# The second half of head 0's keys in one transfer instead of two

## The chip, the cores and the metric

The kernel runs on 1 core of one Trainium2 chip. The metric is the time of one execution on the device in microseconds (us). Before the change it is 656.38 us, the median of 3 runs (656.35 to 656.39).

## What is computed

One token passes through a decoder layer: layer norm, attention over a long cache, and a gated feed-forward block. The part that matters here is the attention. 32 query heads share 8 key-value heads, each with 65536 cached rows of 128 bf16 numbers, 16 MB of keys and 16 MB of values a head:

```python
B, Sq, D = 1, 1, 512
Hq, Hkv, Sk, Dh = 32, 8, 65536, 128
q = (x @ wq).reshape(B, Sq, Hq, Dh).transpose(0, 2, 1, 3)
scores = jnp.einsum("bhqd,bhkd->bhqk", q, k) * (Dh ** -0.5)
p = _softmax(scores, axis=-1)
o = jnp.einsum("bhqk,bhkd->bhqd", p, v)
# then o @ wo, the residual, layer norm, sigmoid(g) * u and the down projection
```

Every byte of the cache is read once.

## The kernel before, in words

**Tiles.** The 16 MB of one head's keys (or values) are 32 chunks. A chunk is 2048 bf16 numbers (4 KB) on each of 128 partitions. Keys and values arrive in `ring`, a buffer of 36 chunks. A load normally brings half a head: 16 chunks, 64 KB on each partition, 8 MB in all. The two halves are called `Kh.0`, `Kh.1`, `Vh.0`, `Vh.1` for head h.

**Engines.** VectorE turns each chunk of keys with one 32x32 block transpose (L531, `ktw<-ring`) into `ktw`, which holds 8 chunks. TensorE then multiplies the query into it, four matmuls a chunk (L443, `PS<-ktw`). It does this in groups of four chunks, and a place in `ktw` is free for the transpose eight chunks later when the scores of its chunk are done. After the 32 chunks of a head comes the softmax: VectorE takes the maxima (L538 and L562 to L568), ScalarE the exponentials (L577) and the next head's query weights (L500). The values are multiplied (L443, `PS<-ring,PT_sb`) during the next head, half a head at a time, after the second and the fourth quarter of that head's keys.

**The order of the loads.** All of them are issued by SyncE (SP) from one list written out by hand, and SP works strictly in its order (L339 to L375). A load that writes over a part of `ring` waits for a mark that the part has been read. The marks of the keys are tiny memsets behind the transposes (L534). In head 0, mark `F0.0` stands after the first 16 chunks and `F0.1` after all 32. In the later heads the marks `Fh.0` and `Fh.1` stand after 12 and 28 chunks. `PVh.r` is the end of the value matmuls in quarter r. The list begins so:

| load | place in `ring` | SP waits for |
|---|---|---|
| `wq` (4 MB, into `ktw`), `K0.0a`, `K0.0b`, `K0.1a`, `K0.1b` (4 MB each) | chunks 0 to 35 | nothing |
| `K1.0` | 0 to 15 | `F0.0` |
| `V0.0` | 20 to 35 | `F0.1` |
| `K1.1` | 4 to 19 | `F1.0` |
| `V0.1` | 20 to 35 | `PV0.1` |
| `K2.0`, then on in the same way | 0 to 15 | `F1.1` |

**Head 0.** Its keys come in four loads of eight chunks, each with a semaphore of its own. `ORDER` (L247) says in which order the chunks are turned: 4 to 15, then 0 to 3, then 16 to 31. So the transposes number s = 0, 4, 16 and 24 of head 0 are the ones that wait for `K0.0a`, `K0.0b`, `K0.1a` and `K0.1b` (L524). Transpose s = 0 waits for the query as well. The later heads have two waits, at s = 0 and s = 16.

Of the kernel before, what the change touches and what calls it, by code (L numbers as in the profile page):

```python
# [35 lines left out]
class Prog:  # L36
# [14 lines left out]
    def op(self, eng, fn, deps=(), name=None, to=None, times=1):  # L51
        assert name is None or name not in self.where, name
        self.ops[eng].append(dict(fn=fn, deps=[d for d in deps if d], name=name, dma=None, to=to, times=times, part=self.part.get(eng)))
        if name:
            self.where[name] = (eng, len(self.ops[eng]) - 1)

    def dma(self, eng, fn, sem, deps=(), name=None):
        self.op(eng, fn, deps, name)
        rec = self.dma_sems.setdefault(sem, dict(sem=None, count=0))
        rec["count"] += 16  # L60
        self.ops[eng][-1]["dma"] = (sem, rec["count"])
# [162 lines left out]
def bass_sequential_preLN__gqa_block_cached__glu_gated_glu__decode_kernel(  # L224
# [22 lines left out]
    with ExitStack() as es:  # L247
# [67 lines left out]
        def ps(bank, c0, c1, p0=0, p1=128):  # L315
            return PS[p0:p1, bank * 512 + c0: bank * 512 + c1]
# [13 lines left out]
        def first_chunk(k, h, q):  # L330
            return AT[{("K", 0): "K0", ("V", HKV - 1): "V7"}.get((k, h), k)][q]

        def load(k, h, q, deps, sem, name, cols=None):
            j0, j1 = PIECES[q]
            a, z = cols or (j0, j1)
            cache = A_k_cache if k == "K" else A_v_cache
            rows = cache[0, h, j0 * TC * 128:j1 * TC * 128, :].rearrange("(p t) d -> p (t d)", p=128)
            at = (first_chunk(k, h, q) - j0) * CH
            dma("sp", lambda e: e.dma_start(ring[:, at + a * CH:at + z * CH], rows[:, (a - j0) * CH:(z - j0) * CH]), sem, deps, name)  # L339

        dma("sp", lambda e: e.dma_start(ktw[:, 0:NKT * CH].rearrange("p (k n) -> p k n", k=4),
                                        A_wq.rearrange("(p k) n -> p k n", p=128)), "r0", (), "wq")
        for q in range(2):
            for i in range(2):
                j0 = 16 * q + 8 * i
                load("K", 0, q, (), f"r{2 * q + i + 1}", f"K0.{q}{'ab'[i]}", (j0, j0 + 8))
        for h in range(1, HKV):
            load("K", h, 0, ["F0.0" if h == 1 else f"F{h - 1}.1"], "ka", f"K{h}.0")
            load("V", h - 1, 0, ["F0.1" if h == 1 else f"PV{h - 2}.3"], "va", f"V{h - 1}.0")
# [164 lines left out]
        def dve_block(b):  # L514
            h, r = b // NR, b % NR
            for c in range(NC):
                n, s = b * NC + c, r * NC + c
                j = ORDER[s]
                q = sum(j >= z for _, z in PIECES)
                at = (first_chunk("K", h, q) + j - PIECES[q][0]) * CH  # L520
                src = ring[:, at:at + CH].bitcast(fp32)
                dst = ktw[:, (n % NKT) * CH:(n % NKT + 1) * CH].bitcast(fp32)
                if h == 0:
                    deps = [f"K0.{q}{'ab'[j % 16 // 8]}"] if s in (0, 4, 16, 24) else []  # L524
                    if s == 0:
                        deps.append("q")
                else:
                    deps = [f"K{h}.{q}"] if s in (0, 16) else []
                if r:
                    deps.append(f"S{b - 1}.{c}")  # L530
                op("dve", lambda e, d=dst, sr=src: e.transpose(d, sr), deps, f"T{b}.{c}", to="T")  # L531
                mark = ({15: 0, 31: 1} if h == 0 else {11: 0, 27: 1}).get(s)
                if mark is not None:
                    op("dve", lambda e, m=4 * h + mark: e.memset(scr[:, m:m + 1], 0.0), (), f"F{h}.{mark}")  # L534
            if b % NR == NR - 1:
                for k in range(NR):
                    u = b - NR + 1 + k
                    op("dve", lambda e, u=u: e.tensor_reduce(M_sb[:, u % 4:u % 4 + 1], ps(u % NS, 0, 512), AX.X, ALU.max),  # L538
                       [f"S{b}.{NC - NR + k}"], f"mx{u}", to="D")
                op("dve", lambda e: e.memset(scr[:, 32 + b // NR:33 + b // NR], 0.0), (), f"G{b // NR}")  # L540
# [255 lines left out]
        for i in range(HKV + 1):  # L796
            loop, last = 0 < i < HKV, i == HKV
            for r in range(NR):
                P.part = {"dve": (f"A{r}", i) if loop else None}
                if not last:  # L800
                    dve_block(NR * i + r)
                    pe_scores(NR * i + r)
                if i and r == 1:
                    P.part = {"dve": ("A4", i) if loop else None}
                    transposed(i - 1)
                    P.part = {"pe": ("V0", i), "dve": ("B0", i) if loop else None}
                    denominators(i - 1)
                    op("pe", lambda e: None, [f"V{i - 1}.0", f"z{i - 1}"])
                    pv(i - 1, r, 6)
                    pv(i - 1, r, 2)  # L810
                if i and r == 3:
                    if last:
                        P.part["pe"] = ("L", i)
                        project7()
                        columns()
                    P.part["pe"] = ("V3", i)
                    op("pe", lambda e: None, [f"V{i - 1}.1"])
                    pv(i - 1, r, 5 if last else 6)
                    if last:
                        P.part["pe"] = ("VL", i)  # L820
                        op("pe", lambda e: None, [f"V{i - 1}.1b"])
                    pv(i - 1, r, 3 if last else 2)
                    P.part["pe"] = ("O", i)
                    head_out(i - 1)
                if not last and r == 3:
                    P.part = {"pe": ("X", i), "dve": ("A3", i) if loop else None}
                    softmax(i)
# [89 lines left out]
```

## Time and profile before

| what | us |
|---|---|
| median of 3 runs | 656.38 (656.35 to 656.39) |
| span of the profiled execution, first to last instruction | 655.0 |
| of the median outside that span | 1.4 |
| TensorE busy in the span | 397.5 |
| VectorE busy | 350.3 |
| ScalarE busy | 43.1 |
| bytes read from HBM | 282.33 MB |

Of the profiled execution the page gives the span, and no other time of its own, so its time is set beside the median as span plus 1.4 us. Times inside the trace are counted from the span's start. PE is TensorE, PEld its weight loads, DVE VectorE, ACT ScalarE, SPq the issuing sequencer of SyncE. In the rows on DMAs the last column is the time from issue to landing, that is until the semaphore of the load is full. In the timelines the columns are start, length, engine, line, operation and tiles.

### The profile page before, as it was taken

The numbers are of one execution on the slowest core, as the hardware profiler recorded it, in microseconds if no ns is written. First come the engines' busy times: TensorE is split into PE (matmuls) and PEld (weight loads), VectorE is DVE, ScalarE is ACT, GpSimd is POOL, SyncE is SP. The second block draws the span as 40 slices with busy tenths as digits, with TensorE's granted clock in tenths as the row PEclk, the third lists the DMA queues.
The fourth block names the chain that finished last, engine by engine and source line by source line (L and its number), as shares of the span: only waits on it lengthen the run. The fifth ranks groups of instructions, "written<-read, shape, count | busy, mean of one in ns | idle before, by whom it ended". The sixth has DMA issues, their size and how long they took to land.

```text
span 655.0 us, 6176 instructions
## 1 busy us (share of the span) xinstructions
PE 397.5 (61%) x2317; PEld 66.7 (10%) x1549; DVE 350.3 (53%) x428; ACT 43.1 (7%) x114; POOL 3.7 (1%) x19
## 2 busy tenths in 40 slices
PE   2778672937548293674828467392845739285466
PEld 1100010110101000010100101010010101001122
DVE  3398853819266290935719184481917548092202
ACT  1100200020000200002000200002000020001101
POOL 1000000000000000000000000000000000000000
PEclk9799695977959687785968769596796958878656
DMA  9999999999999999999999999999999989999998
GB/s 400 432 434 462 424 408 448 448 448 412 420 448 448 432 400 448 448 448 404 428 448 448 436 396 448 448 448 416 416 448 448 448 384 448 448 448 424 417 412 363
DMA packets 6372, 282.33 MB, mean 431 GB/s; under 512 B 738, under 2 KB 868, under 8 KB 1252
## 3 DMA queue, kind: packets, MB, share of 16 engines
q1 hardware_dynamic: 6340, 282.33, 99.7%
q10 hardware_dynamic: 32, 0.00, 0.0%
HBM read 282.33 MB, written 0.00 MB: 431 GB/s over the span
## 4 chain that ended last, share of the span: by engine, by line
DMA 66%; DVE 30%; PE 2%; issue 1%; SPq 0%; PEldq 0%
DMA ring<-in_A_k_cache_dram 58%; DVE ktw L531 30%; DMA ring<-in_B_w_up_dram 4%; DMA ring<-in_A_v_cache_dram 4%; PE PS L443 2%; PE PS L866 0%; PE PS L847 0%; DVE hh L859 0%; DVE hhT L863 0%; SPq L368 0%; SPq L339 0%; DVE y_sb L884 0%; PEldq L171 0%
## 5 line engine op out<-in xcount | busy, mean ns | idle before, releaser
L531 DVE STREAM_TRANSPOSE ktw<-ring 128x1024 f32<-128x1024 f32 x256 | 291.5, 1208 | 165.0 <-DMA ring<-in_A_k_cache_dram 165.0
L443 PE MATMUL PS<-ktw 128*128 128x512 bf16 x1024 | 276.3, 419 | 163.4 <-DVE ktw L531 155.8
L443 PE MATMUL PS<-ring,PT_sb 128*32 x1024 | 85.0, 420 | 55.0 <-issue 46.6
L443 PEld LDWEIGHTS PS<-ktw 128*128 x256 | 26.2, 102 | 401.5 <-issue 234.3
L618 ACT ACTIVATE po_sb<-PS,rl 128x512 bf16<-128x512 f32 x8 | 5.5, 687 | 523.4 <-PE PS L443 523.4
L443 PEld LDWEIGHTS PS<-ring,PT_sb 128*32 x1024 | 20.7, 116 | 117.5 <-issue 116.2
L566 DVE TENSOR_REDUCE gmj<-PS 1x4 f32<-1x128 f32 x8 | 2.2, 278 | 53.5 <-PE PS L564 53.5
L538 DVE TENSOR_REDUCE M_sb<-PS 128x1 f32<-128x512 f32 x32 | 19.9, 683 | 19.3 <-PE PS L443 19.3
L577 ACT ACTIVATE P_sb<-PS,negmax 128x512 bf16<-128x512 f32 x32 | 21.6, 686 | 0.3
L587 DVE STREAM_TRANSPOSE PT_sb<-P_sb 128x512 bf16<-128x512 bf16 x32 | 19.9, 674 | 1.7 <-ACT P_sb L577 1.7
L443 PE MATMUL PS<-ktw,xz 128*8 x32 | 9.6, 476 | 6.1 <-DMA ktw<-in_A_wq_dram 6.1
L634 DVE TENSOR_TENSOR Lw<-O,blk_of 128x896 bf16<-128x896 bf16 (+1 forms) x2 | 1.4, 682 | 15.9 <-ACT O L624 15.9
L489 DVE STREAM_TRANSPOSE qt<-qh 32x512 bf16<-32x512 bf16 x1 | 0.7, 699 | 14.8 <-ACT qh L486 14.8
L571 PE MATMUL PS<-one_f,gmrep 1*128 1x1 f32 x16 | 4.7, 358 | 5.0 <-DVE gmrep L568 5.0
L564 PE MATMUL PS<-identf,gm 128*1 128x128 f32 x16 | 4.5, 380 | 5.1 <-issue 2.9
L643 DVE CAST O<-PS 128x28 bf16<-128x28 f32 (+1 forms) x2 | 0.3, 174 | 12.8 <-PE PS L640 12.8
L577 ACT ACTIVATION_READ_ACCUMULATOR P_sb<-PS,negmax 128x1 f32 x32 | 6.5, 203 | 0.0
L621 PE MATMUL PS<-sel_bf,po_sb 128*128 128x4 bf16 x32 | 2.1, 170 | 6.3 <-ACT po_sb L618 6.3
L504 ACT ACTIVATE PS<-zcol 128x512 f32<-128x512 bf16 x8 | 5.0, 622 | 0.0
L573 ACT ACTIVATE negmax<-PS 128x1 f32<-128x1 f32 x8 | 1.4, 171 | 54.0 <-PE PS L571 54.0
L571 PEld LDWEIGHTS PS<-one_f,gmrep 1*128 1x128 f32 x16 | 4.0, 307 | 8.8 <-DVE gmrep L568 8.8
L592 PE MATMUL PS<-L_sb,lsel 128*128 128x4 f32 x16 | 2.5, 229 | 3.8 <-DVE PT_sb L587 3.8
(90 smaller groups left out, 65.4 us busy)
## 6 DMA issues: line engine op xcount, KB each, us to landing
ring<-in_A_k_cache_dram SPq DMA_DIRECT2D x4, 4096.0 KB, 34.8
ring<-in_A_v_cache_dram SPq DMA_DIRECT2D x1, 5120.0 KB, 30.1
ktw<-in_A_wq_dram SPq DMA_DIRECT2D x1, 4096.0 KB, 12.2
ktw<-in_A_wo_dram SPq DMA_DIRECT2D x1, 3584.0 KB, 18.4
ring<-in_A_v_cache_dram SPq DMA_DIRECT2D x1, 3072.0 KB, 36.9
ring<-in_B_w_gate_dram SPq DMA_DIRECT2D x1, 1792.0 KB, 23.4
ring<-in_B_w_up_dram SPq DMA_DIRECT2D x1, 1792.0 KB, 27.2
ring<-in_B_w_down_dram SPq DMA_DIRECT2D x1, 1024.0 KB, 29.2
```

What stands on the lines that cost most here:

```text
L443: return e.add_instruction(mybir.InstMatmult(name=nc.get_next_instruction_name(), engine=mybir.EngineType.PE, ins=[rhs, lhsT], outs=[e.low ...
L504: op("act", lambda e: e.activation(ps(PO, 0, 512), bass.AP(tensor=zcol, offset=0, ap=[[1, 128], [0, 512]]), AF.Copy), ["zcol"] if h == 0 e ...
L531: op("dve", lambda e, d=dst, sr=src: e.transpose(d, sr), deps, f"T{b}.{c}", to="T")
L538: op("dve", lambda e, u=u: e.tensor_reduce(M_sb[:, u % 4:u % 4 + 1], ps(u % NS, 0, 512), AX.X, ALU.max), [f"S{b}.{NC - NR + k}"], f"mx{u}" ...
L564: op("pe", lambda e: e.matmul(ps(MISC, 0, 128, 0, 1), lhsT=gm[:, :], rhs=identf[:, :], start=True, stop=True), [f"gm{h}"], f"gmT{h}", to="Q")
L566: op("dve", lambda e: e.tensor_reduce(gmj[:, :], ps(MISC, 0, 128, 0, 1).rearrange("p (i a c) -> p a i c", a=4, c=NC), AX.XY, ALU.max), [f" ...
L571: op("pe", lambda e: e.matmul(ps(MISC, 128, 129), lhsT=gmrep[0:1, :], rhs=one_f[0:1, 0:1], start=True, stop=True), [f"gmrep{h}"], f"neg{h}")
L577: op("act", lambda e, b=b: e.activation(P_sb[:, (b % 4) * 512:(b % 4 + 1) * 512], ps(b % NS, 0, 512), AF.Exp, bias=negmax[:, k:k + 1], sca ...
L587: op("dve", lambda e, b=b: e.transpose(PT_sb[:, (b % 4) * 512:(b % 4 + 1) * 512], P_sb[:, (b % 4) * 512:(b % 4 + 1) * 512]), [f"E{b}"], f" ...
L592: op("pe", lambda e: e.matmul(ps(MISC, 132, 136), lhsT=lsel[:, :], rhs=L_sb[:, :], start=True, stop=True), [f"PT{NR * h + NR - 1}"], f"l{h ...
L618: op("act", lambda e: e.activation(po_sb[:, :], ps(PO, 0, 512), AF.Copy, scale=rl[:, :]), [f"PV{h}.{NR - 1}", f"rl{h}"], f"po{h}", to="po")
L621: op("pe", lambda e, t=t: e.matmul(ps(OX, 0, 4), lhsT=po_sb[:, t * 128:(t + 1) * 128], rhs=sel_bf[:, 8 * t:8 * t + 8:2], start=(t == 0), s ...
```

## The change

The two loads `K0.1a` and `K0.1b` become one load of all sixteen chunks. It keeps the name `K0.1a` and its semaphore, and its place in the list. The wait of transpose s = 24 goes, since the wait of s = 16 now stands for the whole half. Everything else is as it was: the places in `ring`, the order of chunks, the marks.

```diff
-        for q in range(2):
-            for i in range(2):
-                j0 = 16 * q + 8 * i
-                load("K", 0, q, (), f"r{2 * q + i + 1}", f"K0.{q}{'ab'[i]}", (j0, j0 + 8))
+        for i in range(2):
+            load("K", 0, 0, (), f"r{i + 1}", f"K0.0{'ab'[i]}", (8 * i, 8 * i + 8))
+        load("K", 0, 1, (), "r3", "K0.1a")
...
                 if h == 0:
-                    deps = [f"K0.{q}{'ab'[j % 16 // 8]}"] if s in (0, 4, 16, 24) else []
+                    deps = [f"K0.{q}{'ab'[j % 16 // 8]}"] if s in (0, 4, 16) else []
```

## The prediction

> **What bounds the kernel now.** I read the page first, then the order of the loads on SP, then VectorE around the change. The page:
>
> ```profile
> DMA  9999999999999999999999999999999989999998
> q1 hardware_dynamic: 6340, 282.33, 99.7%
> ktw<-in_A_wq_dram SPq DMA_DIRECT2D x1, 4096.0 KB, 12.2
> ```
>
> The 16 DMA engines are busy in every slice, with packets in 99.7% of their time. The kernel is as long as its transfers. An engine that waits costs nothing as long as the next load is issued before the queue runs dry, and a microsecond of empty queue can't be won back, because no later idle time of the DMA engines exists. So the question is one only: does a load get issued too late?
>
> The chain of waits, 40 to 130 us, with start and length of each piece:
>
> ```profile
> 45.34 24.98 DMA ring<-in_A_k_cache_dram
> 84.16 24.75 DMA ring<-in_A_k_cache_dram
> 108.93 13.67 DVE ktw L531 x13
> ```
>
> K1.0 is issued at 45.34 and lands at 70.32; K1.1 is issued at 84.16 and lands at 108.91. Next the issues of SP in the timeline, and what the DMA view of single stretches gives from issue to landing (39.3 is the load issued at 2.00, 48.4 the one at 2.60, 26.2 the one at 63.41, 27.4 the one at 100.82):
>
> ```profile
> 2.00 0.56 SPq L339 DMA_DIRECT2D ring<-in_A_k_cache_dram  x1
> ring<-in_A_k_cache_dram SPq DMA_DIRECT2D x1, 4096.0 KB, 39.3
> 2.60 43.08 SPq L339 DMA_DIRECT2D ring<-in_A_k_cache_dram  x2
> ring<-in_A_k_cache_dram SPq DMA_DIRECT2D x1, 4096.0 KB, 48.4
> 63.41 0.33 SPq L339 DMA_DIRECT2D ring<-in_A_v_cache_dram  x1
> ring<-in_A_v_cache_dram SPq DMA_DIRECT2D x1, 26.2
> 100.82 0.33 SPq L339 DMA_DIRECT2D ring<-in_A_v_cache_dram  x1
> ring<-in_A_v_cache_dram SPq DMA_DIRECT2D x1, 27.4
> 122.62 0.33 SPq L339 DMA_DIRECT2D ring<-in_A_k_cache_dram  x1
> ```
>
> So K0.1a lands at 41.3, K0.1b at 51.0, K1.0 at 70.3, V0.0 at 89.6, K1.1 at 108.9, V0.1 at 128.2. From one landing to the next it is 9.7 us for 4 MB and 19.3 us for 8 MB, without a gap. V0.0 is issued 6.9 us before K1.0 lands, K1.1 5.4 us before V0.0 lands. These two leads are what the change touches. VectorE, in the timeline:
>
> ```profile
> 31.65 14.81 DVE L531 STREAM_TRANSPOSE ktw<-ring 128x1024 f32<-128x1024 f32 x13 [2.98 <-DMA ring<-in_A_k_cache_dram]
> 45.24 0.06 DVE L534 MEMSET scr<- 1x1 f32 x1
> 46.39 16.97 DVE L531 STREAM_TRANSPOSE ktw<-ring 128x1024 f32<-128x1024 f32 x15
> 63.30 0.06 DVE L534 MEMSET scr<- 1x1 f32 x1
> 69.23 0.21 DVE L568 COPY gmrep<-gmj 1x128 f32<-1x128 f32 x1
> 70.34 14.93 DVE L531 STREAM_TRANSPOSE ktw<-ring 128x1024 f32<-128x1024 f32 x13 [0.90 <-DMA ring<-in_A_k_cache_dram]
> 84.05 0.06 DVE L534 MEMSET scr<- 1x1 f32 x1
> ```
>
> Between the marks F0.0 (45.24) and F0.1 (63.30) the 16 transposes of the second half run without a stop, 18.06 us or 1.13 us each. When they begin, K0.1a has been there for 3.9 us. When the ninth begins, about 54.3, K0.1b has been there for 3.3 us. VectorE waits for neither.
>
> **The change, part by part.** *Removed: one DMA issue on SP (0.5 us at 2.60) and a wait at s = 24.* Both lie beside work: after its issues SP waits for F0.0 until 45.3, and the wait at s = 24 held nothing up. That is worth 0.
>
> *The transfer itself.* Pairs of 4 MB loads land 9.7 + 9.7 = 19.4 us apart, single 8 MB loads 19.3. The whole half lands where its second part landed, at 51.0; I take 0, within 0.1 either way.
>
> *Moved: the wait of s = 16.* It now ends at 51.0 instead of 41.3. VectorE comes to it at 45.24, so it stands still for 5.7 us. F0.0 is set before that and K1.0's issue at 45.34 stays, so the queue holds K1.0 until 70.3. Behind the waiting transpose stand the other 15, F0.1, the maxima of head 0 and the first transposes of head 1. F0.1 comes at 51.0 + 18.06 = 69.06, and SP issues V0.0 0.11 us after its mark, as at 63.41: at 69.17. That is only 1.15 us before K1.0 lands, where it was 6.9.
>
> *Added: a nearly empty queue before V0.0.* What does a load cost that is issued when the queue has nothing ahead of it? The one instance of its kind is wq, issued at 0.00: 12.2 us to landing for 4 MB, which takes 9.7 in a full queue. So 2.5 us go before and after the data. The other bound is the output, one small store:
>
> ```profile
> 653.82 0.33 SPq L886 DMA_DIRECT2D out_dram<-y_sb  x1
> SPq L221 <- DMA out_dram<-y_sb: 0.8, 1, 0.8
> ```
>
> It is done 0.33 + 0.8 = 1.1 us after its issue. I take 2.5, because wq is a load of megabytes from SP like these, and keep 1.1 as the other end. V0.0 lands at 69.17 + 2.5 + 19.3 = 91.0, 1.4 us later than before (with 1.1: at 89.6, no later).
>
> The Trainium skill ("DMA: Bandwidth & Descriptors", Anatomy of one DMA) gives a fixed part of about 2.0 us for a DMA of the GpSimd path; no run here shows that path. By it V0.0 would land at 90.5.
>
> *The second late load.* The maxima end 69.44 - 63.30 = 6.14 us after F0.1: at 75.2. Head 1's transposes begin then, not at 70.34, as K1.0 has long landed. From their first start to F1.0 it took 84.05 - 70.34 = 13.71. So F1.0 comes at 88.9 and K1.1 is issued at 89.0 instead of 84.16. Two limits hold for its landing. In a full queue it follows V0.0 by 19.3: 110.3. Issued into an empty one: 89.0 + 2.5 + 19.3 = 110.8. With V0.0 landing at 91.0 the lead is 2.0 us, less than the 2.5 that the start takes, so it lies between; I take the middle, 110.55. Against 108.91 that is 1.65 us late. With 1.1 for the start: 89.0 + 1.1 + 19.3 = 109.4, 0.5 late.
>
> *Where it stops.* V0.1 waits for the value matmuls of head 0, issued at 100.82 before. They move with VectorE by 4.8 (89.0 - 84.2) to 5.7 us, to 105.6 to 106.5. K1.1 lands at 110.5, so the lead is 4.0 to 4.9 us against 2.5 needed; no gap. VectorE waited 16.73 us for K1.1:
>
> ```profile
> 108.93 14.81 DVE L531 STREAM_TRANSPOSE ktw<-ring 128x1024 f32<-128x1024 f32 x13 [16.73 <-DMA ring<-in_A_k_cache_dram]
> ```
>
> That idle time swallows its delay. From there all is as before, 1.65 us later: K2.0 issued 13.7 us after K1.1 lands, 5.6 us before V0.1 lands, and so on to the end.
>
> **Sum:** 0 + 0 + 1.4 (V0.0) + 0.25 (K1.1) = 1.65 us. The profiled span of 655.0 becomes 656.65. The median lies 1.4 us above the span; 656.38 + 1.65 gives **658.0 us**.
>
> **The rivals.** *Covered (0.15).* The 1.15 us of lead and a start nearer to the store's 1.1 hide V0.0's delay, and K1.1 costs at most the 0.5 worked out above: 656.4 to 657.2, about 656.8. For it speaks that SP's later issues take 0.33 us against wq's 0.40 and that part of the 2.5 may be due to the kernel's beginning. Against it: wq is the only large load seen to start alone.
>
> *Wider gaps (0.12).* TensorE loses its clock and VectorE waits for it. The first row below shows TensorE's work behind F0.1, 3.0 us long. Behind F0.0 it ends the same way at 48.3, and the next group can begin only when the first transpose after the stop ends, 51.0 + 1.2 = 52.2: 3.9 us idle. The trace has such a place, the windows view from 69.30 to 79.60 (the granted clock is the 0.50), and TensorE there:
>
> ```profile
> 63.41 2.98 PE L443 MATMUL PS<-ktw 128*128 128x512 bf16 x13 [0.75 <-DVE ktw L531]
> 69.30:79.60 10.30, 6.55 (x16) 1.00 (x6) 9.40 (x10) 3.33 (x10) 0.00 (x0) 0.50 1.15 496
> 73.63 14.33 PE L443 MATMUL PS<-ktw 128*128 128x512 bf16 x51 [3.54 <-ACT ktw L500]
> 83.81 0.23 issue
> ```
>
> After 3.54 us of idle time TensorE works at half clock and VectorE loses 0.2 us to it (the last row, from the chain, within the 13.71). In head 1 TensorE now starts 69.06 - 63.30 = 5.76 us later (79.4), the transposes 4.9 us later (75.2), so up to 0.9 us more could be lost ahead of F1.0, and 0.2 ahead of F0.1. K1.1 then lands by 111.9, 3.0 us late: 659.4. Against it: after the stop the transposes have no head start on TensorE, and eight places in `ktw` give 9 us of room.
>
> The Trainium skill ("TensorE: Matmul & The Clock Gate", Part 1: The HAM clock gate) says that an idle window of about 3.4 us halves the clock, and that the windows run freely. The row agrees (0.50 after 3.54 us); by it the stop of 3.9 us halves the clock, or not, by where it lies.
>
> *Faster (0.03).* If every load paid a start of its own even in a full queue, as wq pays 2.5, one load fewer would bring 2.5 us: 653.9. It decides from the point where two 4 MB loads together take longer than one of 8 MB, and where VectorE's new wait stays covered. The rows deny it: K0.1a and K0.1b land 9.7 apart, half of 19.3.
>
> The Trainium skill ("DMA: Bandwidth & Descriptors", Rules for kernel authors) advises large coalesced transfers on the ground of that fixed part; by its 2.0 us the time would be 654.4.
>
> *The change doesn't bite.* If K0.1 came before 45.2 there would be no wait. The queue ahead of it (16 MB at 9.7 us each 4 MB) excludes this.
>
> **How the numbers follow.** The forecast, two thin gaps of 1.0 to 2.4 us in all, gets 0.70; covered 0.15, wider 0.12, faster 0.03. A measurement of this kernel can tell about 0.2%, 1.3 us, from no change. "Slower" is the forecast's part above 1.3 (0.59) and the wider case: 0.71. "Same" is covered and the forecast's lower part (0.11): 0.26. "Faster" 0.03. The range goes from 657.2, where the covered case ends, to 659.2, short of the far end of the wider case; some 0.2 lie outside.
>
> **What the profile after will show.** Right, step by step: VectorE idle for 5.7 us before L531, until about 51.0, released by the key load; F0.1 about 69.1 and V0.0's issue 0.1 behind it; V0.0 landing at 91.0, K1.1 issued about 89.0 and landing at 110.5; all later landings 19.3 apart. Wrong would be: landings still at 89.6 and 108.9 (covered), or a wait of VectorE for TensorE before F1.0 and K1.1's issue after 89.5 (wider), or K0.1 landing well ahead of 51.0 (faster).

## The result, and the profile after

The change makes the kernel slower: 659.56 us (median of 5, 658.79 to 660.30) against 656.38 (now median of 5, 656.35 to 656.97), a ratio of 1.0043 with a 95% interval of 1.0033 to 1.0054. That is 3.2 us, where 1.65 were forecast with a range up to 659.2. The profiled execution itself took 658.83 us with a span of 657.5, 2.5 us more than before, and lies at the short end of the five: their spans are 657.5, 659.0, 658.4, 658.2 and 657.5. So two things have to be explained, the 2.5 us of this profile and the further 0.7 to 1.5 us of other executions.

The page after, of the DMA engines:

```profile
DMA  9999999999999999899998999989999999999998
q1 hardware_dynamic: 6196, 282.33, 99.5%
```

It looks as full as before. 99.5% for 99.7% of a span of 657 us is about 1.3 us more in which engines moved nothing; a share averaged over 16 engines and the whole span hides what matters here.

VectorE's timeline around the stop, three pieces:

```profile
45.34 0.06 DVE L533 MEMSET scr<- 1x1 f32 x1
51.05 1.25 DVE L530 STREAM_TRANSPOSE ktw<-ring 128x1024 f32<-128x1024 f32 x1 [5.65 <-DMA ring<-in_A_k_cache_dram]
...
69.16 0.06 DVE L533 MEMSET scr<- 1x1 f32 x1
...
75.23 1.23 DVE L530 STREAM_TRANSPOSE ktw<-ring 128x1024 f32<-128x1024 f32 x1
```

VectorE stands for 5.65 us until the whole half has landed at 51.02, mark F0.1 comes at 69.16 in place of 63.30, and head 1's transposes start at 75.23 in place of 70.34. Now the issues of SP, and from the DMA view the time to landing of the loads issued at 69.27, 89.13 and 105.95:

```profile
69.27 0.33 SPq L339 DMA_DIRECT2D ring<-in_A_v_cache_dram  x1
89.13 0.33 SPq L339 DMA_DIRECT2D ring<-in_A_k_cache_dram  x1
105.95 0.33 SPq L339 DMA_DIRECT2D ring<-in_A_v_cache_dram  x1
```

```profile
ring<-in_A_v_cache_dram SPq DMA_DIRECT2D x1, 21.7
ring<-in_A_k_cache_dram SPq DMA_DIRECT2D x1, 21.7
ring<-in_A_v_cache_dram SPq DMA_DIRECT2D x1, 24.2
```

V0.0 lands at 91.0 and K1.1 at 110.85, where they landed at 89.6 and 108.9. That is 1.4 us late and then 1.94. V0.1 follows by 19.3, without a gap. In this profile another 0.5 us goes between 246 and 324 us, where three loads took 19.4 to 19.55 us each. So the chain up to K1.1 went as forecast to 0.3 us, and yet most executions are slower than that.

### The profile page after: what moved, and what is told of

It reads as the page before. It is cut to its first block, busy times and chain, and to the rows that moved or that the text cites. A ratio compares the mean times of both kernels' runs of the same rounds, so it can differ in the third digit from the quotient of the medians.

```text
span 657.5 us, 6174 instructions
## 1 busy us (share of the span) xinstructions
PE 400.8 (61%) x2317; PEld 66.7 (10%) x1549; DVE 350.3 (53%) x428; ACT 43.1 (7%) x114; POOL 3.7 (1%) x19
## 3 DMA queue, kind: packets, MB, share of 16 engines
q1 hardware_dynamic: 6196, 282.33, 99.5%
## 4 chain that ended last, share of the span: by engine, by line
DMA 64%; DVE 31%; PE 3%; issue 1%; ACT 1%; SPq 0%; PEldq 0%
DMA ring<-in_A_k_cache_dram 56%; DVE ktw L530 30%; DMA ring<-in_B_w_up_dram 4%; DMA ring<-in_A_v_cache_dram 4%; PE PS L442 2%; ACT P_sb L576 0%; DVE M_sb L537 0%; PE PS L865 0%; PE PS L846 0%; SPq L339 0%; DVE hh L858 0%; DVE hhT L862 0%; PE PS L563 0%; PE PS L570 0%; ACT ktw L499 0%
## 5 line engine op out<-in xcount | busy, mean ns | idle before, releaser
L442 PE MATMUL PS<-ring,PT_sb 128*32 x1024 | 88.0, 432 | 53.2 <-issue 45.6
L537 DVE TENSOR_REDUCE M_sb<-PS 128x1 f32<-128x512 f32 x32 | 19.9, 682 | 19.3 <-PE PS L442 19.3
```

The source lines that it names most:

```text
L442: return e.add_instruction(mybir.InstMatmult(name=nc.get_next_instruction_name(), engine=mybir.EngineType.PE, ins=[rhs, lhsT], outs=[e.low ...
```

## The experiments

Theory 1: the late wait costs, since V0.0 and K1.1 are issued too late, and how late K1.1 is varies with TensorE's clock in head 1. Rivals: the size of the transfer costs; the two gaps add up; VectorE's stop costs in proportion to its length. Theory 2 came with the first profile: later transfers run slower. Theory 3 came with the runs and is told where it arose.

One detail of the trace carries most of what follows. Each load raises its semaphore 16 times. The Trainium skill ("DMA: Bandwidth & Descriptors", Why a DMA increments its semaphore by 16 and not by 1) says that each increment is one DMA engine which has finished its share. The trace fits: a load of 8 MB has 128 packets of 64 KB, each takes 2.42 us in a full queue. By their times the 128 form 16 chains of eight, and 8 x 2.42 = 19.4 us is about the 19.3 us between two landings. The time between the first and the last of the 16 increments tells how far the engines are apart.

### Is it the wait or the size?

*Two loads, one wait* keeps the two transfers of the kernel before and only lets s = 16 wait for both.

```diff
-                    deps = [f"K0.{q}{'ab'[j % 16 // 8]}"] if s in (0, 4, 16, 24) else []
+                    deps = [f"K0.{q}{'ab'[j % 16 // 8]}"] if s in (0, 4, 16) else []
+                    if s == 16:
+                        deps.append("K0.1b")
```

> Two loads of eight chunks as before the change, but the transpose s = 16 waits for both. Theory 1 (the late wait costs: V0.0 and K1.1 are issued too late): as after the change, V0.0 issued at 69.2 and landing at 91.0, K1.1 landing at 110.9, 658.8 to 660.3 us. Rival (the size of the transfer costs, the wait is beside the point): 656.4 us, landings at 89.6 and 108.9.

Measured: 659.44 us (658.23 to 661.34), ratio 1.0053 (1.0039 to 1.0067). K1.1's issue and its time to landing in the profile (span 656.9):

```profile
88.95 0.33 SPq L339 DMA_DIRECT2D ring<-in_A_k_cache_dram  x1
```

```profile
ring<-in_A_k_cache_dram SPq DMA_DIRECT2D x1, 21.8
```

V0.0 lands at 91.3, K1.1 at 110.7. With the size as before and only the wait moved, the time is that of the changed kernel: the size of the transfer is not the cause; waiting for the whole half is.

### Giving the late loads their lead back

*Values in halves*: the change, and V0.0 in two parts, the first of which waits only for chunk 23 of head 0 (a new mark; the first halves of all heads' values are split alike).

```diff
-            load("V", h - 1, 0, ["F0.1" if h == 1 else f"PV{h - 2}.3"], "va", f"V{h - 1}.0")
+            load("V", h - 1, 0, ["F0.2" if h == 1 else f"PV{h - 2}.3"], "va", f"V{h - 1}.0a", (0, 8))
+            load("V", h - 1, 0, ["F0.1"] if h == 1 else (), "va", f"V{h - 1}.0", (8, 16))
```

> The change, and the first half of each head's values loaded in two parts of 4 MB; V0.0's first part waits only for chunk 23 of head 0, so the queue doesn't run dry before V0.0. Theory 1 (K1.1's own issue at 89.1 decides, and its start costs 2.4 us whatever came before): V0.0 lands at 89.7, K1.1 still at 110.8, 658.8 to 660 us. Rival (the two gaps add up, 1.4 and 0.56): K1.1 lands at 109.5, about 657.2 us.

Measured: 659.65 us (658.48 to 659.76), ratio 1.0043 (1.0030 to 1.0056). V0.0 lands at 89.9, with no gap. K1.1:

```profile
89.67 0.33 SPq L339 DMA_DIRECT2D ring<-in_A_k_cache_dram  x1
```

```profile
ring<-in_A_k_cache_dram SPq DMA_DIRECT2D x1, 21.8
```

It lands at 111.5. Its start took 21.8 - 19.3 = 2.5 us, of which 2.25 fell behind the end of the queue at 89.9. Closing the first gap alone gains nothing: the second gets as much wider. The rival in which the gaps add up is out.

*Keys in halves*: the change, and the second half of the keys of heads 1 to 7 in two parts, the first issued after 8 transposes.

```diff
-            load("K", h, 1, [f"F{h}.0"], "kb", f"K{h}.1")
+            load("K", h, 1, [f"F{h}.3"], "kb", f"K{h}.1a", (16, 24))
+            load("K", h, 1, [f"F{h}.0"], "kb", f"K{h}.1", (24, 32))
```

> The change, and the second half of the keys of heads 1 to 7 loaded in two parts of 4 MB, the first of which is issued after 8 transposes in place of 12. Theory 1: K1.1's first part is issued at about 84.5, 6 us before V0.0 lands, and has no gap; V0.0's gap of 1.4 us stays: K1.1 lands at 110.3, 657.9 us, and the runs lie closer together, if their spread comes from VectorE waiting for TensorE in head 1 ahead of F1.0. If the spread comes from the transfers themselves it stays at 1.5 us.

Measured: 659.39 us (658.42 to 659.61), ratio 1.0039 (1.0026 to 1.0052). The spans are 657.1 to 657.9, closer together and lower than those of the changed kernel; the time outside the span rose in two executions to 2.2 and 2.4 us from 1.3, which wasn't followed up. V0.0 lands at 91.45, K1.1 at 110.8, 19.3 behind it: only the first gap is left, and it costs 1.9 us by itself. Closing the second alone doesn't bring K1.1 forward either (110.85 in the changed kernel), so each gap hides the other. That the longest spans are gone once K1.1 has no gap of its own fits with their arising at K1.1. The time expected, 657.9, was 1.5 us too low.

*Both splits together*, for which the diffs are the two above.

> The change with both of these splits: no load is issued late though VectorE still stands for 5.7 us. Theory 1: 656.4 to 656.7 us, landings at 89.7 and 109.0. Rival (the stop of VectorE or the larger transfer costs of itself): 658 us or more.

Measured: 658.12 us (657.32 to 659.62), ratio 1.0026 (1.0015 to 1.0036). V0.0 lands at 89.55 and K1.1 at 108.91, as in the kernel before, though VectorE still stands for 5.7 us. Four of seven spans are 655.8 to 656.2, against 655.0 to 655.6 of the kernel before in the same round. The median lies on the rival's 658 (the stop of VectorE costs of itself), but the landings up to K1.1 don't show such a cost. The profiled execution (657.6) shows a third late load:

```profile
106.63 0.33 SPq L339 DMA_DIRECT2D ring<-in_A_v_cache_dram  x1
```

```profile
ring<-in_A_v_cache_dram SPq DMA_DIRECT2D x1, 23.6
```

V0.1 is issued 2.3 us before K1.1 lands and lands 2.05 us late. Its start cost 23.6 - 19.3 = 4.3 us, more than in an empty queue. The 16 increments of V0.1 are spread over 2.08 us, those of K1.1 over 0.55. So there is a new cause: with a load that comes late, but not too late, some engines fall behind the others.

### Why some executions take longer still

*The changed kernel again*, three more times, each with a profile.

> The changed kernel as it is, for a second profile and five more times beside the others. Theory 1 (late issues, and how late depends on where TensorE's clock windows lie in head 1): the extra time over before is all there when K1.1 lands, and later landings follow 19.3 apart. Theory 2 (the order of the packets is disturbed and later transfers run slower): K1.1 lands near 110.9 as before and the rest is lost in single later loads, as in the first profile, where 0.5 us was lost between 246 and 324.

> The changed kernel once more, for a third profile. Theory 3 (one DMA engine of the sixteen falls behind the others in the load issued late, by up to 1.5 us and by chance, and stays behind to the end, since each engine carries the same bytes): where the span is above 658, the increments of the semaphore of K1.1 are spread over 1.5 to 2 us in place of 0.4 to 0.7, and those of every later load as well; where the span is near 657.4 they are not. Theory 2 (later loads run slower): a long span without such a spread.

> The changed kernel, for a fourth profile. As the third: theory 3 goes by the spread of the sixteen increments in K1.1's landing, theory 2 by single later loads of more than 19.4 us.

Measured: 660.00 us (658.70 to 660.39, 5 runs, ratio 1.0048 with 1.0035 to 1.0062), 659.69 (3 runs) and 658.64 (3 runs). Of the 16 executions, the first profile's five among them, seven have spans of 657.1 to 657.5 and nine of 658.2 to 659.0. The profiles caught two of each kind. K1.1's issue and time to landing, in the profile with span 657.5, then in those with 658.8 and 659.0:

```profile
88.93 0.33 SPq L339 DMA_DIRECT2D ring<-in_A_k_cache_dram  x1
```

```profile
ring<-in_A_k_cache_dram SPq DMA_DIRECT2D x1, 21.7
```

```profile
89.43 0.33 SPq L339 DMA_DIRECT2D ring<-in_A_k_cache_dram  x1
```

```profile
ring<-in_A_k_cache_dram SPq DMA_DIRECT2D x1, 22.8
```

```profile
89.40 0.33 SPq L339 DMA_DIRECT2D ring<-in_A_k_cache_dram  x1
```

```profile
ring<-in_A_k_cache_dram SPq DMA_DIRECT2D x1, 23.1
```

V0.0 lands at 91.1 in the last two. K1.1 lands at 110.7, 112.25 and 112.5. From the traces, the time from the first to the last of the 16 increments of a load, in us (the last column is the first of the two loads of V7's second half):

```
kernel                      span   K1.0  V0.0  K1.1  V0.1 ... V7.1
before                      655.0  0.69  0.68  0.58  0.59     0.46
changed, first profile      657.5  0.61  0.50  0.40  0.38     0.44
changed, second             657.5  0.66  0.71  0.42  0.40     0.37
changed, third              658.8  0.45  0.46  1.58  1.57     1.57
changed, fourth             659.0  0.47  0.61  1.87  1.82     1.63
both in halves              657.6  0.56  0.55  0.55  2.08     2.09
```

In the two long executions the engines part company in K1.1 and stay 1.6 us apart for 520 us. In the trace the packets of K1.1 form 16 chains of eight here too, as in the short executions: the engines that are ahead take over nothing from those that have fallen behind, and the kernel ends with the last one. Theory 2 has a smaller share: between K1.1 and the end the four profiled executions lose 0.4 to 0.8 us more, in single loads of up to 19.7 us.

### Is it TensorE's clock?

The two long profiles issue K1.1 0.3 to 0.5 us later than the two short ones, and in both VectorE waited for TensorE ahead of it, in the short ones not. In all four TensorE works at half clock for 6.8 us in head 1; that ends at 83.3 and 83.7 us in the short profiles and at 84.3 in both long ones. So K1.1 is issued 2.3 and 1.9 us before V0.0 lands in the former, 1.6 and 1.7 in the latter. The waits of VectorE from 76 to 95 us, fourth profile:

```profile
DVE ktw L530 <- PE PS L442: 0.5, 1, 0.5
```

*TensorE kept warm* adds matmuls of zeros to the softmax.

```diff
+            for _ in range(10):
+                op("pe", lambda e: e.matmul(ps(5, 0, 512), lhsT=bass.AP(tensor=zcol, offset=0, ap=[[1, 128], [0, 128]]), rhs=qz[:, 0:512], start=False, stop=False, skip_group_check=True))
             op("pe", lambda e: e.matmul(ps(MISC, 0, 128, 0, 1), lhsT=gm[:, :], rhs=identf[:, :], start=True, stop=True),
...
+            for _ in range(16):
+                op("pe", lambda e: e.matmul(ps(5, 0, 512), lhsT=bass.AP(tensor=zcol, offset=0, ap=[[1, 128], [0, 128]]), rhs=qz[:, 0:512], start=False, stop=False, skip_group_check=True))
```

> The changed kernel with 26 matmuls of zeros added to the softmax of each head on TensorE (10 ahead of the maximum, 16 behind it), so that TensorE isn't idle for 3 us there; the sums that they go into don't change. Theory 1: the granted clock stays at full from 60 to 89, VectorE doesn't wait for TensorE in head 1, K1.1 is issued at 88.9 to 89.1 in every execution, and the spans lie within 0.5 us of 657.0. Theory 2: the spans keep their range of 657 to 659.

Measured: 659.63 us (658.94 to 659.88), ratio 1.0042 (1.0028 to 1.0056), spans 657.6 to 658.4. The windows view shows the granted clock (1.00) held, and the changed kernel's own from 76.90 below it; then K1.1:

```profile
69.00:75.00 6.00, 5.42 (x24) 1.34 (x15) 3.05 (x10) 0.00 (x0) 0.00 (x0) 1.00 0.91 350
75.00:89.00 14.00, 12.35 (x55) 2.74 (x28) 14.00 (x15) 3.33 (x10) 0.00 (x0) 1.00 1.04 449
```

```profile
76.90:83.60 6.70, 4.32 (x11) 0.40 (x3) 6.70 (x7) 2.23 (x7) 0.00 (x0) 0.50 1.08 470
```

```profile
88.75 0.33 SPq L339 DMA_DIRECT2D ring<-in_A_k_cache_dram  x1
```

```profile
ring<-in_A_k_cache_dram SPq DMA_DIRECT2D x1, 23.2
```

VectorE waits for nothing from 76 to 95 us, K1.1 is issued 2.1 us before V0.0 lands at 90.9, and still it lands at 112.0, with increments 2.10 us apart. But this is not a long execution like the two above. Fifteen engines are done at 110.47, as in the short ones; one alone is 1.5 us behind. The page has a queue that no other page has:

```profile
q8 instruction: 1, 0.02, 0.0%
```

This load of 16 KB of instructions runs from 107.72 to 108.64 us. It begins where one engine's seventh packet of K1.1 ends (107.72), and that engine's eighth takes 2.92 us from 108.63 in place of 2.42: 1.4 us of the 1.5. By the other 15 K1.1 would have landed 0.3 us late, as in the short executions. So the run doesn't refute theory 1 in the form of the clock. Nor does it confirm it: the spans of the other four, 657.6 to 658.3, lie above the 656.5 to 657.5 expected, and no trace shows why. The clock remains a candidate for what decides between short and long executions; it is not shown.

### The late issue alone

*V0.0 late, nothing else*: the kernel before, with V0.0's mark set later, behind all four maxima or, with k == 0, behind the first.

```diff
-            load("V", h - 1, 0, ["F0.1" if h == 1 else f"PV{h - 2}.3"], "va", f"V{h - 1}.0")
+            load("V", h - 1, 0, ["L0" if h == 1 else f"PV{h - 2}.3"], "va", f"V{h - 1}.0")
...
+                    if b // NR == 0 and k == 3:
+                        op("dve", lambda e: e.memset(scr[:, 60:61], 0.0), (), "L0")
```

> The kernel before the change, but SP waits for a mark behind the four maxima of head 0 before it issues V0.0: at 68.3, 2.0 us before K1.0 lands, while VectorE and TensorE do nothing else than before, and K1.1 is issued at 84.2. Theory 1 and 3 (the late issue alone costs): V0.0 lands at 90.0 to 90.7, all later loads as much later, 656.8 to 657.5 us, up to 659 where an engine falls behind. Rival (VectorE's stop costs, not the issue): 656.4 us.

> The same with the mark behind the first maximum: V0.0 issued at 66.6, 3.7 us before K1.0 lands. By the 2.5 us of the prediction nothing is lost: 656.4 us in every execution. Theory 3, after the run with 3 us of maxima: some executions lose 0.5 to 2 us here too, since a single engine starts late.

Measured, behind four maxima: 659.32 us (658.80 to 659.73), ratio 1.0039 (1.0026 to 1.0053), spans 657.5 to 658.4. Its profile, issues and time to landing of V0.0:

```profile
68.32 0.33 SPq L339 DMA_DIRECT2D ring<-in_A_v_cache_dram  x1
84.02 0.33 SPq L339 DMA_DIRECT2D ring<-in_A_k_cache_dram  x1
```

```profile
ring<-in_A_v_cache_dram SPq DMA_DIRECT2D x1, 23.7
```

VectorE runs as in the kernel before and K1.1 is issued at 84.02, 8 us before V0.0 lands. One load issued 2.0 us before the queue ends costs as much as the whole change: it lands at 92.0, 2.4 us late, where 90.0 to 90.7 was expected, its increments 1.78 us apart, and they are 2.00 apart in V7.1. The first packets of V0.0 start on the engines between 69.40 and 71.70, 1.1 to 3.4 us after the issue. In the changed kernel, where V0.0 is issued 1.05 us ahead, they start between 70.21 and 71.02, 0.9 to 1.75 us after it. Those first packets are slow as well: the 16 take 3.06 us on average in place of 2.42, all rounds behind them 2.42 again. So of the 2.4 us that this start costs, some 0.6 lie in slow first packets; the prediction's 2.5 had not been taken apart.

Behind the first maximum: 656.95 us (656.33 to 658.05, 11 runs), ratio 1.0007 (0.9998 to 1.0016). The profile (span 655.0):

```profile
66.42 0.33 SPq L339 DMA_DIRECT2D ring<-in_A_v_cache_dram  x1
```

```profile
ring<-in_A_v_cache_dram SPq DMA_DIRECT2D x1, 23.2
```

3.8 us ahead, it lands at 89.64 with increments 0.62 apart: no more than 0.1 us is lost there. The spans of the others go up to 656.1, those of the kernel before in that round to 655.9; the interval doesn't tell the two kernels apart.

### The length of the stop

*Idle maxima* ahead of s = 16 in the kernel before (two loads, both waits), 5 of them and then, with range(20), 20. They write to a tile that is free until the end.

```diff
+                if h == 0 and s == 16:
+                    for st_ in range(5):
+                        op("dve", lambda e, u=st_: e.tensor_reduce(sg2[:, u:u + 1], ps(5, 0, 512), AX.X, ALU.max), ["zy"])
```

> The kernel before the change, two loads and both waits, with five idle maxima of a zero bank (3.0 us of VectorE) ahead of the transpose s = 16. Theory 1 (only what exceeds the leads costs): V0.0 is issued at 66.4, 3.9 us before K1.0 lands, K1.1 at 86.3, 3.3 us before V0.0 lands: no gap, 656.4 to 656.6. Rival (each us that VectorE stands still costs in proportion, as 5.7 us cost 2 to 3): 657.5 to 658.

> The same with twenty maxima, 12.0 us of VectorE. Theory 1: V0.0 is issued at 75.4 and lands 21.7 later at 97.1; K1.1 is issued at 95.4 (12 later than 84.2, less the 0.9 that VectorE waited there) and lands at 117.1, so 8.2 us in all: 664.6 us. Every us of the stop beyond the first six costs one. Rival in proportion to the stop: 661 us.

Measured: 657.96 us (656.63 to 658.64, 11 runs, ratio 1.0014 with 1.0005 to 1.0023) and 667.10 us (666.43 to 668.98, 5 runs, ratio 1.0166 with 1.0152 to 1.0180). The issues of V0.0 and K1.1 and their times to landing, short stop, then long:

```profile
66.36 0.33 SPq L339 DMA_DIRECT2D ring<-in_A_v_cache_dram  x1
87.00 0.33 SPq L339 DMA_DIRECT2D ring<-in_A_k_cache_dram  x1
```

```profile
ring<-in_A_v_cache_dram SPq DMA_DIRECT2D x1, 23.8
ring<-in_A_k_cache_dram SPq DMA_DIRECT2D x1, 23.3
```

```profile
75.26 0.33 SPq L339 DMA_DIRECT2D ring<-in_A_v_cache_dram  x1
94.90 0.33 SPq L339 DMA_DIRECT2D ring<-in_A_k_cache_dram  x1
```

```profile
ring<-in_A_v_cache_dram SPq DMA_DIRECT2D x1, 22.0
ring<-in_A_k_cache_dram SPq DMA_DIRECT2D x1, 21.9
```

The long stop does what the sum says: V0.0 starts in an empty queue and takes 22.0, 2.7 us more than its 19.3; the profiled span is 663.1, 8.1 us longer. (The median of 667.10 is 2.5 us above the 664.6 expected. Some 2 of them lie outside the span, 3.3 to 3.6 us here, 1.3 before, which wasn't followed up.) The short stop should have cost nothing by a need of 2.5 us, as the leads are 3.9 and 3.1 us. By K1.1's landing it cost 1.4 us in the profile, 0.5 in V0.0 and 0.9 in K1.1, and its increments are 1.71 us apart from K1.1 on. The spans go from 655.3 to 657.3. The rival in proportion gave 657.5 to 658 and would fit the median; it fails at the long stop, and at V0.0 late, where VectorE doesn't stop at all.

### All late loads together

From the profiles: how long before the load ahead of it landed a load was issued (its lead), and by how much its own landing was later than 19.3 us after that one.

```
lead  late   load, kernel
6.9   0.0    V0.0, before
5.5   0.0    K1.1, before
4.9   0.0    V0.1, changed, first profile
4.7   0.0    V0.1, keys in halves
3.9   0.5    V0.0, short stop
3.8   0.1    V0.0 behind the first maximum
3.1   0.9    K1.1, short stop
2.3   0.2    K1.1, changed, second profile
2.3   0.2    K1.1, two loads, one wait
2.3   0.3    K1.1, long stop
2.3   2.05   V0.1, both in halves
2.1   1.8    K1.1, TensorE warm (0.3 without the engine held up by instructions)
2.0   2.4    V0.0 behind four maxima
1.9   0.55   K1.1, changed, first profile
1.7   2.15   K1.1, changed, fourth
1.6   1.9    K1.1, changed, third
1.05  1.4    V0.0, changed, first profile
1.0 to 1.1, 1.5 to 1.7: V0.0 in the six other profiles where it is issued so
0.25  2.25   K1.1, values in halves
```

Nothing is lost from 4.7 us up. Around 1 us the loss is even. Between about 1.5 and 4 us a load loses 0.1 to 2.4 us, with leads alike and results apart. The packets show where that is decided. Of the nine loads with leads of 1.6 to 2.3 us, four landed 21.7 to 21.9 us after their issue; in them all 16 engines had begun 1.8 to 2.0 us after it. Four others took 22.8 to 23.7 us; in them the last engine began 2.5 to 4.1 us after the issue. (The ninth is the one with the load of instructions.)

## Why the prediction was wrong

*What bounds the kernel: right, with one thing missing.* The DMA queue sets the time and lost time isn't won back. But "a microsecond of empty queue" was thought of one queue. It is sixteen engines, and the time is that of the one that lost most.

*The transfer itself: right.* It landed at 51.02; the two loads with one wait cost the same.

*The moved wait: right.* F0.1 at 69.16 (forecast 69.06), V0.0 issued at 69.27 (69.17).

*V0.0 in a nearly empty queue: right.* 91.0 forecast, 91.0 to 91.2 in the four profiles. Loads that found the queue empty, or about to be, took 2.7 (long stop) and 2.5 us (values in halves) for the start, against 2.5 taken from wq. That the price is slow first packets in part doesn't touch the sum.

*The second late load: this step failed.* K1.1's issue was forecast at 89.0 and came at 88.9 to 89.4. The step then said "the lead is 2.0 us, less than the 2.5 that the start takes, so it lies between; I take the middle, 110.55". It took a full queue and an empty one for the two bounds. They are none: a load issued some 2 us ahead can land later than one issued into an empty queue, 22.8 to 23.7 us after its issue against 21.8 to 22.0, because some engines begin it late. K1.1 landed at 110.85 and 110.7 in the short executions, 0.1 to 0.3 us after the forecast, and at 112.25 and 112.5 in the long ones, 1.7 to 1.95 after it. The long ones are nine of 16, and the median is one of them. So this term, put at 0.25 us, is most of the missing 1.5 us.

*Where it stops: right, but for 0.4 to 0.8 us* that later loads lost in all four profiles; what slowed them stays open. V0.1's lead of 4.9 us held. The same sum had "4.0 to 4.9 us against 2.5 needed"; the need is larger than 2.5, as the short stop shows, and with both halves V0.1's lead of 2.3 was the one that cost.

*The rivals.* Covered fell with the first landing. Faster fell with the landing at 51.02. Wider had the right size of time (up to 659.4) by half of a mechanism: VectorE did lose 0.4 to 0.5 us to TensorE at half clock in two of four profiles, the long ones, and K1.1 was issued at 89.4 there. But its price was the later issue alone. K1.1 landed 1.4 to 1.8 us later than in the short ones for an issue 0.3 to 0.5 us later, and that surplus of 1.1 to 1.5 us, engines that begin late, is not in it. (It also put the half clock down to 3.54 us of idle time; in the trace of the kernel before, the clock had fallen at 69.4, ahead of that idle time, which runs from 70.1 to 73.6.)

What stays open is why a nearly empty queue reaches some engines later than an empty one does, and whether the 0.3 to 0.5 us between K1.1's issues in the short and the long profiles, and TensorE's clock behind them, decide which it will be. K1.1's leads speak for it: 1.9 us and more in the short ones, 1.7 and less in the long ones. V0.0 behind four maxima, at 2.0, and V0.1 with both halves, at 2.3, lost more than 2 us, so the lead alone is not the rule. Nor was it tried whether the changed kernel comes back to 656.4 with the third lead restored as well.

## What to carry to other kernels

Where the DMA queue bounds a kernel, a load's lead (landing of the load ahead minus its own issue) is the number to keep, and here 3.9 us were not always enough and 4.7 were, about twice the 2.5 to 2.7 us that a start in an empty queue cost. Merging two transfers merges their waits: ask who works on the first part, and which later loads are released by that work. Where times of one kernel scatter, look at how far the 16 increments of a load's semaphore lie apart: here an engine that fell behind once was behind until the end. And look at every queue of the page before a run is taken as a refutation: one load of instructions made K1.1 land as late as in a long execution.

## What the runs showed of the hardware that was not expected

A load issued 1.6 to 2.3 us before the queue ended took 22.8 to 23.7 us to land in four of nine cases and 21.7 to 21.9 in four others, where one issued into an empty queue took 22.0. In one of the four slow cases its first packets started over 2.3 us (69.40 to 71.70) instead of 0.8. The spread of 1.6 to 2.1 us between the engines that arose there was still 1.6 to 2.1 us some 500 us later. The first packets of the 16 engines took 3.0 to 3.1 us on average where the queue had run dry, and 2.42 in a full one. A 16 KB load of instructions that fell into a load (107.72 to 108.64 us) put one engine 1.5 us behind the others.
